# A state-space scan beside windowed attention: attention weights turned by DMA, local states evicted into their final place, and a new order of issue

## The chip, the cores and the metric

The kernel runs on one core of a Trainium2 chip. Times are device microseconds (us) of that core. The kernel before took 139.39 us, the median of three runs (138.95 to 139.60). A core has engines with queues of their own: TensorE (PE) for matmuls, VectorE (DVE), ScalarE (ACT), GpSimd (POOL) and SyncE (SP), which here only issues DMAs. Each engine works through its own instructions in the order in which they were issued, and waits on semaphores for the others.

## The reference

Two independent layers over 2048 positions of width 448, whose outputs stand side by side.

```
A: Lam_bar = exp(dt * Lam); B_bar = ((Lam_bar - 1) / Lam)[:, None] * Bmat
   h[t] = Lam_bar * h[t-1] + x[t] @ B_bar.T            (448 complex states, 2048 steps)
   y = 2 * (h @ Cmat.T).real + x * Dskip
B: q, k, v = split(x @ wqkv)                           (16 heads of 28)
   logits[s, w] = q[s] . k[s - 2w] / sqrt(28),  w = 0..7;  -1e9 where s - 2w < 0
   o = sum_w softmax(logits)[w] * v[s - 2w];    out = o @ wo
```

## The kernel before

Position s is written as (p, j) with s = 16 p + j: 128 chunks p, 16 places j in each. Most tiles hold one of them on the partitions, and j in the free dimension.

**Layer B.** x is loaded with transposing DMAs and projected to queries and keys on PE, with the chunks in the free dimension (`prep`). For half b of the places (8 each), `qk` builds products query × key on DVE, two windows at a time. `summ` (L658) sums them per head on PE into `logits`, a PSUM tile with eight windows of 128 columns; its partition is 32 i + 16 r + h for place i, group parity r and head h. Products pass through three buffers. `softmax(b)` then runs a chain: a mask matmul, the maximum over windows on DVE (`top`, L694), its subtraction on PE, the exponential on ACT, the sum over windows on PE (`tot`, L708), and reciprocal and scaling on DVE (`norm`, L713). The weights then have heads on the partitions, while the weighted sum needs chunks there. So `tr` (L720) turns the eight windows by eight PE transposes into a PSUM tile, and `ev` (L725) copies it to `attn` with two ACT copies. `v_proj` makes v per place and evicts it to `vd`, on ACT or DVE; `halo` (L773) shifts rows of `vd` by one chunk with DMAs for places before the first. `pv` multiplies weights and v and adds on DVE (L818, L821), the main work of DVE in the second half; `trd` (L855) transposes a group's result by DMA, or PE does for the last group (`tr`, L864), and PE multiplies with wo.

**Layer A.** Seven blocks m of 64 complex states. `scan` projects x (`bf`, `br`) into four PSUM tiles per block, one per residue i of the place modulo 4, and combines them in a logarithmic scan of matmuls with powers of the transition (`powers` on DVE, L1181) and ACT evictions between them. The projections of residues 0 and 2 are local states: they are evicted to a buffer `eP` (`evP`, L1250, or `evp`, L1253), used by `s1` (L1256), added back into PSUM through an identity matmul (`back`, L1322) once the carry is known, completed by `s6` and `s7`, and evicted for good into `h` (L1336, L1339). `h` has a tile of its own for m < 3; for m = 3 to 6 it lies over the queries of B. `outputs` multiplies h with C, adds the skip term, and evicts into a ring of eight rows for the output DMAs.

**Order.** A planner collects units (an engine, a cost, a function, what they depend on). When the list `ORDER` (L48) has as many entries as there are units, `run` (L130) issues the units in that order: an entry is the unit's number as created, and adding 1000 picks the second of two allowed engines. That order is the order in every engine's queue. Semaphores come from the data that the instructions touch.

SP's queue holds all loads: B's x and weights, A's x (L980, last at L983 to L984), C (L1006), wo (L402), halos, wo's second copy (L407), the Dskip row for A's skip term (L949, L951), the transpose of C (L1010), then transposes of results and the outputs. DVE's queue runs the projections' evictions, then products, `top`, `norm`, and `pv` with `powers` between its steps.

Of the kernel before, what the change touches and what calls it, by code (L numbers as in the profile page):

```python
# [9 lines left out]
ACT = mybir.ActivationFunctionType  # L10
# [28 lines left out]
NF = 3  # L39
WARM = 6  # L40
# [4 lines left out]
HOLD = (0, 0, 0, 1, 0, 0, 7)  # L45
YG = ((3,), (7,), (11,), (1, 5), (9,), (0, 4), (8,), (2, 6), (10,), (12, 13), (14,), (15,))
# [159 lines left out]
class Ctx:  # L206
# [41 lines left out]
    def consts2(self):  # L248
# [22 lines left out]
        def masks():  # L271
            G.memset(mrow[:], 0.0)
            G.affine_select(out=mrow[:], in_=mrow[:], compare_op=ALU.not_equal, fill=-1e9,
                            base=-3, pattern=[[1, 4]], channel_multiplier=1)
# [42 lines left out]
class PartB:  # L317
# [262 lines left out]
    def qk(self, b, prio):  # L580
# [8 lines left out]
        for g in (2 * b + 1, 2 * b):  # L589
            par = g - 2 * b  # L590
            j0 = 4 * g
            for tp in (3, 2, 1, 0):
# [65 lines left out]
                def summ(g=g, tp=tp, par=par, ub=ub, head=first):  # L658
# [5 lines left out]
                    zs = slice(H - H * par, 3 * H - H * par)  # L664
                    for kt in range(3):
                        for i in range(4):
                            nc.tensor.matmul(lg[32 * i:32 * i + 32, 2 * tp:2 * tp + 2, :],  # L667
                                             lhsT=cx.Z[:, kt, zs], rhs=pr[:, :, i, kt, :],
                                             start=(new and kt == 0), stop=(kt == 2), skip_group_check=True)
                    if tp < 2:  # L670
                        for z, t2 in ((cx.Z[:, 3, zs], tp + 2), (cx.Zh[:, zs], tp)):
                            for i in range(4):
                                nc.tensor.matmul(lg[32 * i:32 * i + 32, 2 * t2:2 * t2 + 2, :],
# [16 lines left out]
    def softmax(self, b, prio):  # L690
# [29 lines left out]
        def tr():  # L720
            pt = box["pt"] = self.psum.tile([NCH, W, 2, 4, H], bf16, name="pt_at", tag="s")
            for w in range(W):
                nc.tensor.transpose(pt[:, w].rearrange("q r i h -> q i r h"), box["a"][:, w, :], cx.ident[:])

        def ev():  # L725
            at = self.attn[b] = pool.tile([NCH, W // 2, 2, 2, 4, H], bf16, name="attn%d" % b)
            for x in range(2):
                nc.scalar.copy(at[:, 2 * x:2 * x + 2].rearrange("q z r y i h -> q y (z r) (i h)"),
                               box["pt"][:, 4 * x:4 * x + 4].rearrange("q (y z) r i h -> q y (z r) (i h)", y=2))
# [6 lines left out]
        u = P.add("PE", pe(8, 128), tr, [u], -1, acq="s", rel="at")  # L736
        self.u_attn[b] = P.add("ACT", 2 * act(512), ev, [u], -1, rel="s")

    def v_proj(self, prio, deps):
# [42 lines left out]
        for i0, i1 in ((10, 14), (6, 10), (2, 6), (0, 2)):  # L782
            z = P.add("POOL", 0.9, lambda i0=i0, i1=i1: zero(i0, i1), deps, prio[0])
# [5 lines left out]
    def pv(self, b, prio, deps):  # L789
# [12 lines left out]
        lasts = {}  # L802
        for r in (1, 0):
            last = getattr(self, "pv_last", None)
            us = (5, 4, 1, 0)
            for n in range(4):

                def step(n=n, r=r, part=0):
# [13 lines left out]
                    if n == 0:  # L822
                        mul(0)
                        mul(1)
# [3 lines left out]
                    elif 2 * b + r > 0:  # L828
                        add(3)
                        V.tensor_tensor(acc[:, n1:2 * n1], acc[:, 0:n1], acc[:, n1:2 * n1], op=ALU.add)  # L830
# [16 lines left out]
            if not hasattr(self, "u_first"):  # L847
                self.u_first = last
# [723 lines left out]
```

## Time and profile before

| what | us |
|---|---|
| median of three runs | 139.39 |
| the profiled execution | 139.57 |
| its span, first to last instruction | 137.9 |
| PE busy | 132.2 |
| DVE busy | 123.9 |
| ACT busy | 89.9 |
| POOL busy | 17.4 |

The profiled execution takes 1.7 us more than its span, for what lies around the instructions. Busy time counts an engine as busy while any of its instructions is under way; matmuls overlap, and their ends are modelled, so a busy PE is not one at its peak. A line such as `52.05 0.50 PE L1242 ... x2 [0.32 <-DMA ...]` of the timeline says when instructions of one kind started, how long they took together, where they stand in the program, how many they are, and how long the engine had been idle before, with what ended that idle time. The granted TensorE clock is 1.00 in this execution.

### The profile page before, as it was taken

How to read it: one execution, taken by the hardware profiler on the slowest of the kernel's cores; microseconds unless marked ns; L12 is line 12 of the kernel's file. 1: busy time of each engine (PE TensorE's matmuls, PEld its weight loads, DVE VectorE, ACT ScalarE, POOL GpSimd, SP SyncE). 2: the span in 40 equal slices, each digit the busy share in tenths (PEclk: the TensorE clock that was granted, in tenths of full speed). 3: DMA queues.
4: the chain of work that ended last, by engine and by line, in shares of the span. 5: the costliest groups of instructions: out<-in, count | busy, mean ns of one | idle time of the engine just before them, and what ended most of it. 6: DMA issues, size and time to landing. Idle time of an engine off the chain costs nothing.

```text
span 137.9 us, 2856 instructions
## 1 busy us (share of the span) xinstructions
PE 132.2 (96%) x1080; PEld 69.1 (50%) x1087; DVE 123.9 (90%) x135; ACT 89.9 (65%) x202; POOL 17.4 (13%) x69
## 2 busy tenths in 40 slices
PE   7999989999999998999999999999999999999990
PEld 2644334544555453656534664554665655445750
DVE  1379999899999999999999999999999999999950
ACT  3365588998553975856685899887746352463571
POOL 7489810018000000000000000000000000000000
PEclk9999999999999999999999999999999999999999
DMA  4968953564744337835799109800000462917554
GB/s 129 266 129 212 175 89 39 126 159 109 73 95 86 77 71 125 150 69 143 226 190 221 50 0 96 208 0 2 0 5 0 110 156 37 236 56 238 195 168 140
DMA packets 39582, 16.05 MB, mean 116 GB/s; under 512 B 31573, under 2 KB 38932, under 8 KB 39569
## 3 DMA queue, kind: packets, MB, share of 16 engines
q1 hardware_dynamic: 39506, 15.87, 53.6%
q8 instruction: 8, 0.13, 0.4%
q14 instruction: 5, 0.04, 0.1%
q10 hardware_dynamic: 63, 0.01, 0.0%
HBM read 4.32 MB, written 3.67 MB: 58 GB/s over the span
## 4 chain that ended last, share of the span: by engine, by line
PE 56%; SPq 34%; ACT 3%; issue 2%; DMA 2%; ACTq 0%
PE y_ps L1435 15%; SPq L980 14%; SPq L362 10%; PE scb L1233 6%; PE wo_ps L894 5%; PE scp L1233 3%; PE wo_ps L901 2%; PE scb L1292 2%; DMA xaT_sb<-in_A_x_dram 2%; PE scP L1233 2%; PE y_ps L1431 2%; PE scb L1257 2%; SPq L341 2%; SPq L365 2%; PE logits L667 1%
## 5 line engine op out<-in xcount | busy, mean ns | idle before, releaser
L818 DVE TENSOR_TENSOR prods<-attn,vd 128x3584 bf16<-128x3584 bf16 x12 | 24.1, 2020 | 0.0
L821 DVE TENSOR_TENSOR rb<-rb,prods 128x3584 bf16<-128x3584 bf16 x11 | 22.2, 2021 | 0.1
L652 DVE TENSOR_TENSOR prods<-qk 128x3072 bf16<-128x3072 bf16 (+1 forms) x15 | 19.2, 1328 | 0.3 <-PE logits L667 0.3
L1435 PE MATMUL y_ps<-Ccat,qk 128*128 128x448 bf16 x60 | 15.1, 353 | 0.1
L215 ACT CAST qk<-wo_ps 128x448 bf16<-128x448 f32 (+1 forms) x16 | 8.2, 528 | 10.1 <-PE wo_ps L894 6.5
L477 PE MATMUL qk_ps<-rb 128*128 128x512 bf16 x60 | 14.4, 379 | 0.4 <-DMA rb<-in_B_x_dram 0.4
L215 ACT CAST vd<-v_ps 128x448 bf16<-128x448 f32 x15 | 7.4, 539 | 5.8 <-PE v_ps L763 4.5
L1435 PE MATMUL y_ps<-Ccat,h 128*128 128x448 bf16 x45 | 11.0, 353 | 0.0
L1233 PE MATMUL scb<-xaT_sb,Bcat 128*128 128x512 bf16 x42 | 10.9, 381 | 0.0
L1233 PEld LDWEIGHTS <-Bcat 128*128 128x128 bf16 x84 | 7.6, 100 | 6.4 <-issue 0.2
L1285 ACT CAST ubuf<-scb 128x64 bf16<-128x64 f32 x35 | 7.1, 218 | 5.6 <-PE scb L1292 3.5
L763 PE MATMUL v_ps<-rb 128*128 128x448 bf16 x48 | 9.9, 353 | 0.0
L217 ACT ACTIVATE qk<-qk_ps 64x512 bf16<-64x512 f32 (+1 forms) x15 | 8.9, 599 | 1.0 <-PE qk_ps L484 0.5
L656 DVE TENSOR_TENSOR prods<-qk 128x768 bf16<-128x768 bf16 (+3 forms) x18 | 9.1, 569 | 0.3 <-ACT qk L215 0.2
L477 PEld LDWEIGHTS <-rb 128*128 128x128 bf16 x60 | 5.7, 98 | 7.3 <-issue 1.0
L1435 PEld LDWEIGHTS <-qk 128*128 128x128 bf16 x60 | 5.9, 98 | 5.3
L818 DVE TENSOR_TENSOR rb<-attn,vd 128x3584 bf16<-128x3584 bf16 x4 | 8.1, 2021 | 0.1
L894 PE MATMUL wo_ps<-wo_p,rb 128*128 128x448 bf16 x36 | 8.1, 354 | 0.0
L1183 DVE TENSOR_TENSOR pw<-Dm,spair 128x1920 bf16<-128x1920 bf16 x7 | 8.1, 1153 | 0.0
L215 ACT CAST qk<-qk_ps 128x512 bf16<-128x512 f32 (+2 forms) x11 | 6.3, 585 | 2.5 <-PE qk_ps L484 1.1
L1233 PE MATMUL scp<-xaT_sb,Bcat 128*128 128x512 bf16 x30 | 7.9, 380 | 0.0
L667 PE MATMUL logits<-prods,Zsel 128*32 128x256 bf16 x192 | 7.4, 274 | 0.0
(198 smaller groups left out, 263.1 us busy)
## 6 DMA issues: line engine op xcount, KB each, us to landing
out_dram<-qk SPq DMA_DIRECT2D x32, 112.0 KB, 1.8
vd<-vd SPq DMA_DIRECT2D x3, 392.0 KB, 4.4
rb<-in_B_wqkv_dram SPq DMA_DIRECT2D x3, 336.0 KB, 4.5
qk<-in_A_x_dram SPq DMA_DIRECT2D x1, 448.0 KB, 4.9
ra<-in_A_B_re_dram SPq DMA_DIRECT2D x1, 392.0 KB, 4.1
ra<-in_A_B_im_dram SPq DMA_DIRECT2D x1, 392.0 KB, 5.8
rb<-in_A_C_re_dram SPq DMA_DIRECT2D x4, 98.0 KB, 2.8
rb<-in_A_C_im_dram SPq DMA_DIRECT2D x4, 98.0 KB, 3.1
```

What stands on the lines that cost most here:

```text
L215: nc.scalar.copy(out, in_)
L362: nc.sync.dma_start(self.xT[:, j], bass.AP(x.tensor, x.offset + j * D - DT, [[T * D, NCH], [1, KT * NCH]]), transpose=True)
L477: nc.tensor.matmul(out(n), lhsT=w(n, full, k), rhs=self.xT[:, j:j + 4, k, :], start=(not rfirst and k == 1), stop=(rfirst and k == KT - 1) ...
L652: V.tensor_tensor(out.rearrange("p i j k q -> p i (j k) q"), qq.unsqueeze(1).to_broadcast([NCH, 2, 4 * nk, NCH]), bass.AP(kk.tensor, kk.of ...
L656: V.tensor_tensor(jk(out[:, i, a:e]), qq, kk, op=ALU.mult)
L763: nc.tensor.matmul(box["ps"][:].rearrange("p h d -> p (h d)"), lhsT=self.xT[:, j, k, :], rhs=self.wv[:, k, :], start=False, stop=(k == KT ...
L818: V.tensor_tensor(tmp[i].rearrange("p (j d h) -> p j d h", j=8, d=DH), aa, self.vd[:, o:o + 8], op=ALU.mult)
L821: V.tensor_tensor(acc, acc, tmp[i], op=ALU.add)
L894: nc.tensor.matmul(ps[:], lhsT=self.oTd[g][:, a + kt], rhs=self.wo_p[:, 5 * e + kt, :], start=False, stop=(kt == 2), skip_group_check=True)
L980: nc.sync.dma_start(self.xT[:, j], bass.AP(x.tensor, x.offset + j * D, [[T * D, NCH], [1, KT * NCH]]), transpose=True)
L1233: mt(box[i], lhsT=self.Bcat[:, k, m, :], rhs=self.xk(slice(i, None, 4), k), start=(i % 2 == 0 and k == 0), stop=False, **kw)
L1435: nc.tensor.matmul(ps, lhsT=h, rhs=self.Ccat[:, m, :], start=(m == 0 and not skip), stop=(m == NM - 1), skip_group_check=True)
```

## The change

**Logits.** The eight windows are stored in another order within `logits`, so that a pair of windows stands two apart; the mask follows. Matmuls, columns and banks stay as they are.

**Attention weights.** `tr` and `ev` are replaced by `turn`: per half, one transposing DMA on SP from the scaled weights (128 partitions, 8 windows of 128) into `attn`. `attn` gets the layout that this DMA writes, and the multiplication in `pv` reads it with other strides.

**Local states.** `evP` and `evp` write into rows 0 and 2 of `h`; `s1` and `back` read them there; the final evictions write the same rows. The buffer `eP` is gone.

**Switches.** `ADD` and `EADD` would let POOL DMAs with accumulation replace some additions. All their entries are zero, and `half` is None, so no instruction comes of them.

```
@@ qk.summ @@
+                    at = lambda t, i: lg[32 * i:32 * i + 32, 4 * (t // 2) + t % 2:4 * (t // 2) + t % 2 + 3:2, :]
...
-                            nc.tensor.matmul(lg[32 * i:32 * i + 32, 2 * tp:2 * tp + 2, :],
+                            nc.tensor.matmul(at(tp, i),
...
@@ softmax @@
-        def tr():
-            pt = box["pt"] = self.psum.tile([NCH, W, 2, 4, H], bf16, name="pt_at", tag="s")
-            for w in range(W):
-                nc.tensor.transpose(pt[:, w].rearrange("q r i h -> q i r h"), box["a"][:, w, :], cx.ident[:])
-
-        def ev():
...
+        def turn():
+            at = self.attn[b] = pool.tile([NCH, W, 4, 2, H], bf16, name="attn%d" % b)
+            nc.sync.dma_start(at[:].rearrange("q w i r h -> q w (i r h)"), box["a"][:].rearrange("p w q -> p (w q)"), transpose=True)
...
-        u = P.add("PE", pe(8, 128), tr, [u], -1, acq="s", rel="at")
-        self.u_attn[b] = P.add("ACT", 2 * act(512), ev, [u], -1, rel="s")
+        self.u_attn[b] = P.add("SP", 1.3, turn, [u], -1, rel="at", lat=3.0)
@@ pv.step.mul @@
-                        aa = self.attn[b][:, 2 * (u // 4) + u % 2, r].rearrange("q y i h -> q (y i) h").unsqueeze(2).to_broadcast(
+                        w0 = 4 * (u // 4) + 2 * (u % 2)
+                        aa = self.attn[b][:, w0:w0 + 2, :, r, :].rearrange("q y i h -> q (y i) h").unsqueeze(2).to_broadcast(
@@ scan @@
-            def evp(n, box=box, etile=etile):
-                nc.scalar.copy(etile()[:, n, :], box[2 * n])
+            def evp(n, box=box, hget=hget):
+                nc.scalar.copy(hget()[:, 2 * n, :], box[2 * n])
...
-                mt(box[1 + 2 * i], lhsT=L(1), rhs=box["eP"][:, i, :], start=False, stop=True, **kw)
+                mt(box[1 + 2 * i], lhsT=L(1), rhs=hget()[:, 2 * i, :], start=False, stop=True, **kw)
...
-                mt(box[2 * n], lhsT=cx.ident[:], rhs=box["eP"][:, n, :], start=True, stop=False, **kw)
+                mt(box[2 * n], lhsT=cx.ident[:], rhs=hget()[:, 2 * n, :], start=True, stop=False, **kw)
```

**Order.** There is one unit less per half, so later unit numbers shift. Up to the last load of A's x on SP and the same point on the other engines the order is as before. Behind it:

- SP, before: C, wo, halo of places 0–2, wo's second copy, Dskip (layout for the diagonal), halos 10–14 and 2–6, transpose of C, halo 6–10, transpose of group 3, then the Dskip row and x for the last four places of A, then outputs with the transposes of groups 2 and 1. After: Dskip (diagonal), wo, halos 0–2 and 10–14, the turn of half 1, C, halo 6–10, wo's second copy, transpose of C, transpose of group 3, x for the last places, halo 2–6, the turn of half 0, outputs and the other two transposes. The Dskip row goes out behind the output of place 10 of A.
- DVE, before, from the last eviction of keys: products (group, windows pair) 3/0, 3/1, 2/2, 2/0, 2/1, 1/3, `top` of half 1, an eviction of v (place 1), 0/3, 1/2, `norm` of half 1, 1/1, 0/1, 0/0, 1/0, 0/2, `powers` of block 3, `top` of half 0, `pv`. After: 2/0, 3/0, 2/1, 2/2, 3/1, 1/1, `top` of half 1, 1/3, 1/0, `powers` 3, 0/0, 0/1, 0/2, `norm` of half 1, 0/3, 1/2, `top` of half 0, `pv`. The eviction of v for place 1 is on ACT. Further on, `norm` of half 0 and `powers` of block 5 stand a few steps later in `pv`.
- PE: sums of products follow the products' new order; `tot` of half 1 stands behind the first steps of blocks 0 and 1 of the scan instead of ahead of them; blocks 2 and 3 alternate more closely, and block 4 is finished beside block 6; at the end the wo matmuls of place 7 stand behind the first closing transposes.
- ACT follows; the evictions of places 11 and 7 of B stand behind the first closing one.

More of the change, by code (lines that the diff above doesn't have):

```diff
@@ L39 @@
 NF = 3
+NC = 3
 WARM = 6
@@ L45 @@
 HOLD = (0, 0, 0, 1, 0, 0, 7)
+ADD = (0, 0, 0, 0, 0, 0, 0)
+EADD = (0, 0, 0, 0)
 YG = ((3,), (7,), (11,), (1, 5), (9,), (0, 4), (8,), (2, 6), (10,), (12, 13), (14,), (15,))
@@ L272, in masks @@
             G.memset(mrow[:], 0.0)
-            G.affine_select(out=mrow[:], in_=mrow[:], compare_op=ALU.not_equal, fill=-1e9,
-                            base=-3, pattern=[[1, 4]], channel_multiplier=1)
+            v = mrow[:].rearrange("p (z y) -> p y z", z=2)
+            G.affine_select(out=v, in_=v, compare_op=ALU.not_equal, fill=-1e9,
+                            base=-3, pattern=[[2, 2], [1, 2]], channel_multiplier=1)
             G.memset(mcol[:], 1.0)
@@ L782, in v_proj @@
         for i0, i1 in ((10, 14), (6, 10), (2, 6), (0, 2)):
-            z = P.add("POOL", 0.9, lambda i0=i0, i1=i1: zero(i0, i1), deps, prio[0])
+            z = P.add("POOL", 0.9, lambda i0=i0, i1=i1: zero(i0, i1), [*deps, *self.u_pad.values(), self.u_pad3, self.u_pad3b], prio[0])
             h = P.add("SP", 1.45, lambda i0=i0, i1=i1: halo(i0, i1), [self.u_v[i + 2] for i in range(i0, i1)],
@@ L801, in pv, with step @@
         n1 = 4 * D
-        lasts = {}
+        self.oTd = getattr(self, "oTd", {})
+        lasts, halves, trs = {}, {}, {}
         for r in (1, 0):
             last = getattr(self, "pv_last", None)
+            half = getattr(self, "u_half", None)
+            ahead = half is not None
             us = (5, 4, 1, 0)
             for n in range(4):
-                def step(n=n, r=r, part=0):
+                def step(n=n, r=r, part=0, half=half):
                     alloc()
@@ L822, in step @@
                     if n == 0:
+                        mul(1 if half else 0)
+                        mul(2 if half else 1)
+                    elif n == 1 and half:
+                        mul(3)
                         mul(0)
-                        mul(1)
+                    elif n == 2 and half:
+                        add(1)
+                        add(2)
                     elif n < 3:
@@ L829, in step @@
                         add(3)
-                        V.tensor_tensor(acc[:, n1:2 * n1], acc[:, 0:n1], acc[:, n1:2 * n1], op=ALU.add)
+                        if not EADD[2 * b + r]:
+                            V.tensor_tensor(acc[:, n1:2 * n1], acc[:, 0:n1], acc[:, n1:2 * n1], op=ALU.add)
                     else:
@@ L834, in pv @@
                 dd = []
-                for u in us[:2] if n == 0 else us[n + 1:n + 2] if n < 3 else ():
+                for u in us[:2 + ahead] if n == 0 else us[n + 1 + ahead:n + 2 + ahead] if n < 3 else ():
                     o = j0 + 4 * r + DIL * u
@@ L846, in pv, with merge @@
             self.pv_last = last
+            g = 2 * b + r
+            halves[g] = self.u_half = None
+            if EADD[g]:
+                def merge(g=g):
+                    acc = self.acc[g]
+                    nc.gpsimd.dma_start(acc[:, n1:2 * n1], acc[:, 0:n1], accum_op=ALU.add)
+                halves[g] = self.u_half = P.add("POOL", 1.1, merge, [last], PRI["wo"], lat=3.5)
             if not hasattr(self, "u_first"):
                 self.u_first = last
-        self.oTd = getattr(self, "oTd", {})
-        trs = {}
         for r in (1, 0):
@@ L858, in trd @@
                     nc.sync.dma_start(t, self.acc[g][:, n1:2 * n1], transpose=True)
-                trs[r] = P.add("SP", 1.7, trd, [lasts[r][1]], PRI["wo"], lat=3.6)
+                trs[r] = P.add("SP", 1.7, trd, [halves[g] or lasts[r][1]], PRI["wo"], lat=3.6)
         for j in range(j0, j0 + JB):
@@ L1305, in ev3, with carry @@
                 nc.scalar.copy(hget()[:, 3, 0:384], box[3][:, 0:384])
-            def carry(out, lt, Sc, hv):
-                mt(out[:, 0:NCH], lhsT=lt, rhs=Sc, start=False, stop=True, **kw)
+            def carry(out, lt, Sc, hv, new=False):
+                mt(out[:, 0:NCH], lhsT=lt, rhs=Sc, start=new, stop=True, **kw)
                 mt(out[:, NCH:512], lhsT=lt, rhs=hv[:, 3, 0:384], start=False, stop=True, **kw)
@@ L1390, in scan @@
             done[m] = P.add("POOL", 0.0, lambda: None, [w0, w2, u1], rel=("fl", "pw"), lat=0.0)
+            if add:
+                w0 = w2 = P.add("POOL", 1.2, addin, [w0, w2], pc, rel="cP", lat=3.0)
             self.u_h.append((w0, u1, w2, [u3, eh]))
```

61 lines of the change are left out of this document (33 added, 28 removed), and 56 rows, old and new, of the table ORDER.

## The prediction

> **What bounds the kernel now.** I read the page first: busy shares, then the chain that ended last.
>
> ```profile
> span 137.9 us, 2856 instructions
> PE 132.2 (96%) x1080; PEld 69.1 (50%) x1087; DVE 123.9 (90%) x135; ACT 89.9 (65%) x202; POOL 17.4 (13%) x69
> PE 56%; SPq 34%; ACT 3%; issue 2%; DMA 2%; ACTq 0%
> ```
>
> TensorE (PE) and VectorE (DVE) are both nearly full, so the page alone does not say which sets the end. The chain has two halves: SyncE's queue (SPq 34%) first, PE afterwards. Next I read the timeline of each engine where the halves meet and where the kernel ends (columns: start, duration, engine, line, operation, count; idle time before it in brackets).
>
> ```profile
> 49.11 1.28 SPq L980 DMA_TRANSPOSE xaT_sb<-in_A_x_dram  x1
> 52.05 0.50 PE L1242 MATMUL scb<-xaT_sb,Bcat 64*128 64x512 bf16 x2 [0.32 <-DMA xaT_sb<-in_A_x_dram]
> ...
> 98.02 0.73 PE L1435 MATMUL y_ps<-Ccat,h 128*128 128x448 bf16 x3
> ...
> 127.16 2.09 DVE L833 TENSOR_TENSOR rb<-rb,prods 128x1792 bf16<-128x1792 bf16 x2
> 128.09 1.49 PE L1435 MATMUL y_ps<-Ccat,S 128*128 128x448 bf16 x7
> 129.41 1.50 PE L870 MATMUL pt_o<-ident,rb 128*128 128x128 bf16 x24
> 134.43 0.53 ACT L215 CAST qk<-wo_ps 128x448 bf16<-128x448 f32 x1 [0.22 <-PE wo_ps L901]
> ```
>
> Two things are to be seen. At 52.05 PE waits for the last load of A's x, whose order the change keeps: PE time lost before that point is partly absorbed there. At the end, DVE's last add finishes at 129.25, PE's last y matmul at 129.58, and the closing work (pt_o, wo, eviction) starts from both. After 52 us the two engines thus run to the same finish; a gain on one alone is worth only what the other allows. So I costed DVE and PE apart.
>
> ```profile
> 52.10:65.20 13.10, 12.89 (x171) 7.57 (x174) 12.62 (x16) 8.72 (x27) 0.00 (x0) 1.00 0.65 123
> 97.00:118.00 21.00, 20.95 (x160) 12.25 (x161) 20.74 (x13) 9.79 (x21) 0.00 (x0) 1.00 0.29 52
> 65.20:129.30 64.10, 63.62 (x40) 1.00 0.46 105
> ```
>
> (Windows. The first two rows give length, then busy time and count of PE, PEld, DVE, ACT, POOL, the clock, DMA share, GB/s; the third gives DVE alone.) From 65.2 to 129.3 DVE idles 0.48 us in all: its finish is fixed by when the first weighted product starts. That start is the number to find.
>
> **The change, part by part.**
>
> *Removed from PE and ACT.* Per half of the sequence, eight transposes and two copies.
>
> ```profile
> 56.81 0.61 PE L723 MATMUL pt_at<-ident,attn_t 128*128 128x128 bf16 x8
> 57.64 1.08 ACT L728 COPY attn<-pt_at 128x512 bf16<-128x512 bf16 x2
> ```
>
> The eight transposes stand 0.45 us apart from the next work in the chain of waits (0.61 shown, their ends overlap), so PE saves 2 × 0.45 = 0.9 us and ACT 2 × 1.08 = 2.2 us. ACT is 65% busy; its saving is worth nothing by itself.
>
> *Local states written to their final place.* The evictions at L1251 and L1254 keep their count and shape and only change destination; the final eviction overwrites them after the matmuls that read them, as it already followed those. States 3 to 6 lie over the queries, whose last reader ended at 62.77 (below), before their first eviction. Cost 0 to 0; the switches ADD and EADD are all zero, so what they guard issues nothing.
>
> *The attention turn on SP.* One DMA per half moves 128 × 1024 elements, eight 128 × 128 blocks. No such DMA is in this trace; its nearest rows:
>
> ```profile
> xaT_sb<-in_A_x_dram SPq DMA_TRANSPOSE x16, 2.9
> rb<-rb SPq DMA_TRANSPOSE x3, 3.9
> Ccat<-rb SPq DMA_TRANSPOSE x1, 6.2
> vd<-vd SPq DMA_DIRECT2D x3, 392.0 KB, 4.4
> ```
>
> (Last number: median microseconds from issue to landing.) Four blocks land in 2.9, fourteen in 3.9, twenty-eight in 6.2. The bounds are 2.9 and 6.2; I take 3.9, the row with the same source memory and the nearer size. That is 3.9/14 = 0.28 us per block with all fixed latency included. The Trainium skill (VectorE: DVE Perf Modes, "The three transpose paths") gives 1309 ns for one such block by DMA against 390 ns on TensorE, and advises TensorE where PSUM will do; by it eight blocks in turn would take an estimated 10.5 us. The three rows contradict that as a price per block in a row of them.
>
> When can it be issued? SP in the new order does, after A's x: the Dskip row loads (3 DMAs), wo (8), halo 0–2, halo 10–14, then the turn, then C, which is moved behind it.
>
> ```profile
> 50.50 2.71 SPq L1006 DMA_DIRECT2D rb<-in_A_C_re_dram  x4
> ...
> 56.02 5.31 SPq L402 DMA_DIRECT2D wo_p<-in_B_wo_dram  x8
> 61.42 0.58 SPq L776 DMA_DIRECT2D vd<-vd  x1
> 62.05 0.98 SPq L777 DMA_DIRECT2D vd<-vd  x1
> ...
> 64.39 0.46 SPq L949 DMA_DIRECT2D dsk_raw<-in_A_Dskip_dram  x1
> 64.91 0.53 SPq L951 DMA_DIRECT2D dsk_raw<-in_A_Dskip_dram  x2
> 65.47 0.55 SPq L776 DMA_DIRECT2D vd<-vd  x1
> 66.07 0.86 SPq L777 DMA_DIRECT2D vd<-vd  x1
> ```
>
> From 50.5: Dskip 1.05, wo 5.4, halos 1.6 and 1.5 give 60.1. Landing 60.1 + 3.9 = 64.0 (63.0 to 66.3). C goes out from about 61 instead of 50.5 and is needed by the first y matmuls at 98.02: some 30 us of cover for its loads and its own transpose. The second turn: between its weights and their first reader stand five DVE instructions of 2.02 (row of 65.16 below), 10 us, so 3.9 is covered by 6. While SP waits for those weights, the output of j = 14 and the transpose of group 2 stand behind; the latter needs a later add anyway.
>
> *DVE's order from 30.4 to the first weighted product.*
>
> ```profile
> 30.41 1.90 DVE L656 TENSOR_TENSOR prods<-qk 128x768 bf16<-128x768 bf16 x3 [0.21 <-ACT qk L215]
> 44.60 0.61 DVE L219 CAST vd<-v_ps 128x448 bf16<-128x448 f32 x1
> 45.45 3.70 DVE L656 TENSOR_TENSOR prods<-qk 128x768 bf16<-128x768 bf16 x6
> 58.60 1.76 DVE L652 TENSOR_TENSOR prods<-qk 128x3072 bf16<-128x3072 bf16 x1 [0.31 <-PE logits L667]
> 61.02 1.75 DVE L652 TENSOR_TENSOR prods<-qk 128x3072 bf16<-128x3072 bf16 x1
> 62.69 1.15 DVE L1183 TENSOR_TENSOR pw<-Dm,spair 128x1920 bf16<-128x1920 bf16 x1
> 63.34 0.50 PE L667 MATMUL logits<-prods,Zsel 128*32 128x256 bf16 x12
> 63.77 0.20 PE L286 MATMUL logits<-mrow,mcol 128*128 128x4 bf16 x2
> 64.02 1.22 DVE L696 TENSOR_REDUCE mx<-logits 128x128 bf16<-128x1024 f32 x1 [0.17 <-PE logits L286]
> 65.16 2.02 DVE L818 TENSOR_TENSOR rb<-attn,vd 128x3584 bf16<-128x3584 bf16 x1
> ```
>
> The same instructions run between 30.4 and 65.16 in another order, less one: the eviction of v for j = 1 goes to ACT (44.60 to 45.13, so −0.53). The product now first (r = 0, windows 7 and 6) needs keys of half 1 alone, so the wait of 0.21 goes. The 0.31 goes too, as TensorE's sums now stand closer behind their products. What comes: in the old order the power build (62.69, 1.15 long) lay between the last product and the second maximum and covered its logits on PE. It now runs earlier, and the maximum follows the last product directly. Old distance 62.77 to 64.02 = 1.25, with a backlog of sums on PE; the new one has one sum (twelve matmuls, a 0.50 row) and the mask (0.20), with a handover either side: I take 0.95, bounds 0.7 and 1.25. Against the old idle 0.17 that is +0.78 (0.53 to 1.08). Second, the row sums of half 1 on PE move behind the first steps of scan blocks 0 and 1. Those cannot start before the 52.05 of the x loads and took up to the transposes at 56.81 in the old trace, while DVE reaches the reciprocal at about 57.1: a wait of 0 to 0.6, I take 0.3.
>
> Sum for DVE: −0.53 − 0.21 − 0.31 + 0.78 + 0.3 = 0.0 (−0.5 to +0.6). The first weighted product stays at 65.2. Back from it: maximum 1.14, wait 0.95, two products 3.65; so the weights are ready for the turn at about 59.5, SP is free at 60.1, and the turn lands at 64.0. It is hidden, with 1.2 us to spare. If that cover were gone, each microsecond would go to the end in full. The reads at L818 keep runs of 16 elements and get another stride between them: I count nothing, 0 to 0.
>
> *PE after 52.* It is released at the second maximum by the same products, so it stands level there, then saves the second 0.45. Also the wo matmuls of j = 7 move behind the first closing transposes:
>
> ```profile
> 128.33 0.97 ACT L215 CAST qk<-wo_ps 128x448 bf16<-128x448 f32 x2 [1.63 <-PE wo_ps L894]
> ```
>
> Three matmuls 0.19 apart (seven of the same width in the 1.49 at 128.09) are 0.56. The first closing transposes come at 129.41 − 0.45 − 0.56 = 128.4, just as DVE's first half of the last add is done. PE no longer holds the end up; DVE does. From the last add, I lay the closing steps out with the durations of the old ones (eight transposes 0.45, as 24 in 1.50; four wo matmuls 0.75; evictions 0.53): the last eviction ends 5.3 us after it, against 134.96 − 129.25 = 5.7 before. That is −0.4. ACT has two more evictions in this tail (j = 11 and 7, 0.53 each); they fit between the steps.
>
> The Dskip row for the final y now goes out behind the output of y 10, whose matmuls stand some 8 us of PE work before the closing transposes; with its eviction that puts the issue near 122.7. Before, it landed in 4.9:
>
> ```profile
> rb<-in_A_Dskip_dram SPq DMA_DIRECT2D x1, 112.0 KB, 4.9
> 129.17 1.08 DVE L1412 TENSOR_TENSOR qk<-qk,rb 128x1792 bf16<-128x1792 bf16 x1
> ```
>
> At 127.6 it is there 1.5 us before its reader.
>
> *Sum.* 0.0 on DVE, −0.4 at the end: span 137.5, and the profiled execution's 139.57 becomes 139.2. That execution lies 0.18 above the median of the runs, 139.39; against the median I forecast 139.0. With 0.5% (0.7 us) as what a measurement can tell, that is no change, leaning faster.
>
> **The rivals.**
>
> *Denser than counted.* The waits I put in at the maximum and the reciprocal come to 0.7 and 0, so DVE gains 0.55, and the tail 0.4: 138.4. For it: PE gives up 0.9 and ACT 2.2 in the scan stage, where ACT steps wait for PE and back. Against it: one sum must still run after the last product.
>
> *The turn lands late (slower).* Its bytes go out on the same queue behind a halo of 392 KB whose kind takes 4.4 us. If landing takes more than 5.1 us from its issue, DVE waits, and the surplus goes to the end; the sum changes sign from 5.5. With 6.2, the row of Ccat, and one more microsecond of queueing it lands at 67.3: +2.1 − 0.4 = 140.9 or so; at 6.2 alone, 139.9. For it: the halo ahead. Against: the fourteen-block transposes took 3.9. The Trainium skill (DMA: Bandwidth & Descriptors, "Queues, rings and completion order") says that a DMA's semaphore write lands only after every earlier write of that DMA engine; by that rule the halo's last bytes delay the turn, which speaks for this rival, and no run here isolates it yet.
>
> *Each block in turn.* If the eight blocks cost 1.31 us each, as mechanism a serial walk through blocks, landing is 70.6 and DVE starts 5.4 late: 144. The skill's page above would have it so; 0.28 per block in the row of rb says no.
>
> *PE becomes the bound.* The scan blocks 2 and 3 now alternate, 4 ends later. If PE's gaps between 65 and 128 grow by 1.9 us or more, the end follows PE: 140 and up.
>
> *It doesn't do what it says.* The transposes removed were fill for PE while ACT worked, and PE just waits instead: then only the tail moves, which is my sum with 0.2 less: 139.2.
>
> **How the numbers follow.** My sum, with the last rival, 50%, own range 138.4 to 139.6; of it 15 points lie beyond 0.5% faster. Denser 21%, nearly all beyond 0.5%. Late turn 17%, PE bound 9%, serial blocks 3%: of these 26 points beyond 0.5% slower, 3 within. So faster 0.36, same 0.38, slower 0.26. The range 137.9 to 140.6 takes in the denser case and half of the late ones.
>
> **What would show it.** Right: no pt_at at L723, two DMA transposes into attn landing in 3 to 4.5 us; the first product from attn at 64.8 to 65.8 with no wait for a DMA; DVE idle near 1 us before its second maximum; the first pt_o before 128.8. Wrong: DVE's first read of attn released by the DMA (late turn), PE idle in the scan rows and y matmuls running past DVE's last add (PE bound), or L818 no longer at 2.02 us.

## The result

The changed kernel takes 140.1 us (median of 6 runs, 139.79 to 140.38), against 139.43 us for the kernel before beside it (6 runs, 138.95 to 139.74): ratio 1.0051, 95% interval 1.0027 to 1.0075. It is slower by about half a per cent. The profiled execution took 140.0 us, with a span of 138.3. Three of the four runs of one experiment below (C ahead of the turn) were taken at a lower granted clock, 0.974 to 0.988, than all other runs of this study (0.995 or more), and are not compared with them.

The page of the changed kernel, the same three lines as were shown of before:

```profile
span 138.3 us, 2835 instructions
...
PE 131.3 (95%) x1065; PEld 67.2 (49%) x1071; DVE 123.0 (89%) x134; ACT 88.3 (64%) x199; POOL 17.7 (13%) x69
...
DVE 39%; PE 38%; SPq 9%; issue 5%; ACT 3%; DMA 3%; DVEq 0%; ACTq 0%
```

PE, DVE and ACT all do less than before (PE 131.3 against 132.2, DVE 123.0 against 123.9, ACT 88.3 against 89.9), and yet the span is 0.4 us longer. The chain of work that ended last has changed: PE 56% and SyncE's queue 34% before, now DVE 39% and PE 38%. This does not yet say where the time goes; the timeline has to. The next rows are the changed kernel's timeline, for the places on which the prediction's steps rested, then its waits on SyncE's queue and its DMA issues.

```profile
56.82 0.95 DVE L720 RECIPROCAL rsum<-sm_ps 128x128 f32<-128x128 f32 x1
59.13 1.50 SPq L727 DMA_TRANSPOSE attn<-attn_t  x1
63.51 1.22 DVE L701 TENSOR_REDUCE mx<-logits 128x128 bf16<-128x1024 f32 x1 [0.80 <-PE logits L290]
64.65 2.02 DVE L819 TENSOR_TENSOR rb<-attn,vd 128x3584 bf16<-128x3584 bf16 x1
...
126.48 2.09 DVE L841 TENSOR_TENSOR rb<-rb,prods 128x1792 bf16<-128x1792 bf16 x2
```

```profile
SPq L727 <- DVE attn_t L722: 5.4, 2, 3.9
```

```profile
attn<-attn_t SPq DMA_TRANSPOSE x1, 3.1
```

The front of the kernel went as forecast, or a little better. The first weighted product starts at 64.65 (65.16 before), no DMA holds it up, and the last add ends at 126.48 + 2.09 = 128.57 instead of 129.25: in this pair of traces DVE has gained 0.68 us. Kernels with the same front differ by up to 0.5 us here (in the nine traces of this study with the new front the last add ends between 128.44 and 128.93, in the three with the old one between 128.90 and 129.25), so the gain is rather 0.5, the difference of the means. The loss is behind that point. The timeline of the changed kernel's tail (three engines; columns as before):

```profile
121.25 1.50 PE L1462 MATMUL y_ps<-Ccat,S 128*128 128x448 bf16 x7
...
127.63 0.51 PE L884 MATMUL pt_o<-ident,rb 128*128 128x128 bf16 x6
128.63 0.29 PE L884 MATMUL pt_o<-ident,rb 128*128 128x128 bf16 x2 [0.49 <-DVE rb L841]
128.76 0.73 PE L908 MATMUL wo_ps<-wo_p,rb 128*128 128x448 bf16 x3
129.32 0.61 PE L884 MATMUL pt_o<-ident,rb 128*128 128x128 bf16 x8
130.46 0.92 PE L915 MATMUL wo_ps<-wo_p,rb 128*128 128x448 bf16 x4 [0.52 <-ACT qk L218]
131.21 0.61 PE L884 MATMUL pt_o<-ident,rb 128*128 128x128 bf16 x8
131.98 0.61 PE L884 MATMUL pt_o<-ident,rb 128*128 128x128 bf16 x8 [0.17 <-DVE qk L1474]
...
128.49 1.08 DVE L1439 TENSOR_TENSOR qk<-qk,rb 128x1792 bf16<-128x1792 bf16 x1
129.78 2.15 DVE L1474 TENSOR_TENSOR qk<-y_ps,qk 128x448 bf16<-128x448 f32 x3 [0.20 <-DVE qk L1439]
...
128.96 0.59 ACT L889 CAST rb<-pt_o 128x512 bf16<-128x512 f32 x1 [3.89 <-PE pt_o L884]
129.44 0.97 ACT L218 CAST qk<-wo_ps 128x448 bf16<-128x448 f32 x2
134.94 0.53 ACT L218 CAST qk<-wo_ps 128x448 bf16<-128x448 f32 x1 [0.23 <-PE wo_ps L915]
```

The same stretch before, of PE and DVE:

```profile
130.75 0.92 PE L901 MATMUL wo_ps<-wo_p,rb 128*128 128x448 bf16 x4
131.51 0.61 PE L870 MATMUL pt_o<-ident,rb 128*128 128x128 bf16 x8
...
130.46 2.15 DVE L1447 TENSOR_TENSOR qk<-y_ps,qk 128x448 bf16<-128x448 f32 x3 [0.20 <-DVE qk L1412]
```

From the end of the last add to the end of the last eviction, the tail, are 135.47 − 128.57 = 6.90 us; before there were 5.71, and the forecast said 5.3. DVE's gain and the tail's loss of 1.19 together make the half microsecond of the traces. In this stretch PE, which had no gap there before, stands idle three times (0.49, 0.52, 0.17), and ACT stands idle for 3.89 us ahead of the first closing eviction, with the eviction of j = 11, whose wo matmuls were done at 127.67, queued behind it.

### The profile page after: what moved, and what is told of

It is laid out like the page before. It is cut to its first block, busy times and chain, and to the rows that moved or that the text cites. A ratio compares the mean times of both kernels' runs of the same rounds, so it can differ in the third digit from the quotient of the medians.

```text
span 138.3 us, 2835 instructions
## 1 busy us (share of the span) xinstructions
PE 131.3 (95%) x1065; PEld 67.2 (49%) x1071; DVE 123.0 (89%) x134; ACT 88.3 (64%) x199; POOL 17.7 (13%) x69
## 4 chain that ended last, share of the span: by engine, by line
DVE 39%; PE 38%; SPq 9%; issue 5%; ACT 3%; DMA 3%; DVEq 0%; ACTq 0%
DVE rb L822 11%; DVE prods L819 11%; SPq L366 6%; PE v_ps L760 6%; PE scb L1247 5%; DVE rb L819 4%; PE scp L1247 4%; PE logits L672 3%; DMA rb<-in_B_x_dram 3%; DVE pw L1197 2%; PE qk_ps L481 2%; DVE prods L656 2%; PE wo_ps L915 2%; DVE rb L838 2%; ACT qk L218 1%
## 5 line engine op out<-in xcount | busy, mean ns | idle before, releaser
L819 DVE TENSOR_TENSOR prods<-attn,vd 128x3584 bf16<-128x3584 bf16 x12 | 24.0, 2018 | 0.0
L1462 PE MATMUL y_ps<-Ccat,qk 128*128 128x448 bf16 x60 | 14.6, 352 | 0.0
L218 ACT CAST vd<-v_ps 128x448 bf16<-128x448 f32 x16 | 7.9, 540 | 5.2 <-PE v_ps L760 4.9
L218 ACT CAST qk<-y_ps 128x448 bf16<-128x448 f32 (+1 forms) x9 | 5.6, 663 | 8.2 <-issue 4.2
```

Of the source, the lines that this page charges most:

```text
L218: nc.scalar.copy(out, in_)
L819: V.tensor_tensor(tmp[i].rearrange("p (j d h) -> p j d h", j=8, d=DH), aa, self.vd[:, o:o + 8], op=ALU.mult)
L1462: nc.tensor.matmul(ps, lhsT=h, rhs=self.Ccat[:, m, :], start=(m == 0 and not skip), stop=(m == NM - 1), skip_group_check=True)
```

## The experiments

Four theories. **1**, the order of ACT's queue: the evictions of j = 11 and 7 stand behind the first closing eviction, and ten evictions in a row then set the tail. **2**, a dependency that the data does not need: the transposes of place 1 read columns up to 960, the last add is cut at 896, so two of them wait for the wrong half (the 0.49). **3**, banks of PSUM, the memory into which PE writes: this kernel gives six banks in turn to PE's results, and a result keeps its bank until another engine has evicted it, that is, copied it out. y of places 15 and 14 hold banks until DVE evicts them, after the last add and the Dskip product (x times Dskip for the last places), and closing work (transposes and wo of places 0 to 3) has to wait for these. **4**, the turn or the states in place cost something themselves.

For reading the diffs, units of the order list: 586 and 587 are the transposes and eviction of place 1, 591 and 592 of place 2, 597 and 598 of place 3, 581 and 582 of place 0; 588 is the closing wo of place 1; 555 and 556 are eviction and output of j = 11, 613 to 615 wo, eviction and output of j = 7; 682 are the seven matmuls of y 15, 683 its eviction, 676 and 680 those of y 12/13 and y 14. Line numbers of the experiments are shifted by some lines.

**j = 11's eviction ahead**

```diff
-    675, 554, 586, 587, 555, 556, 613, 614, 615, 591, 592,
+    675, 554, 555, 556, 586, 587, 613, 614, 615, 591, 592,
```

> Only the eviction and the output of j = 11 are moved ahead of the first closing transposes and their eviction. Theory 1 (the order of ScalarE's queue): in the changed kernel j = 11's wo result is ready at about 127.6, but its eviction stands behind the first closing eviction, for which ScalarE idles 3.89 us; moved, it runs in that idle time, ScalarE's tail is one eviction of 0.53 us shorter, and the time falls by about 0.5 us to 139.6. Theory 2 (the last two of the first closing transposes wait for the wrong half of the last add) and theory 3 (the y evictions on VectorE hold the banks of PSUM): no change, within 0.2 us.

Measured: 139.81 us (12 runs), ratio to before 1.0031 (1.0012 to 1.0049). ACT's row of this eviction moved into the idle stretch as planned; the first closing wo did not move with it. Timeline of this run:

```profile
130.56 0.92 PE L918 MATMUL wo_ps<-wo_p,rb 128*128 128x448 bf16 x4 [0.52 <-DVE qk L1477]
...
129.88 2.15 DVE L1477 TENSOR_TENSOR qk<-y_ps,qk 128x448 bf16<-128x448 f32 x3 [0.20 <-DVE qk L1442]
```

The wait is again 0.52, and with ACT's work gone the row now names another releaser: DVE's y eviction.

**j = 7's wo, eviction and output ahead as well**

```diff
-    675, 554, 586, 587, 555, 556, 613, 614, 615, 591, 592,
+    675, 554, 555, 556, 613, 614, 615, 586, 587, 591, 592,
```

> As the run before, and j = 7's wo matmuls, eviction and output are moved ahead too, as the kernel before had them. Theory 1: two evictions (1.1 us) leave ScalarE's tail, and TensorE's wait of 0.52 us for a bank that j = 7's eviction gives back goes: last eviction ends near 134.2 instead of 135.47, time about 138.9 (-1.2). Theory 2: the first closing transposes still wait for the second half of the last add, so at most -0.4. Theory 3: no change, within 0.2 us.

Measured: 139.73 us (12 runs), ratio 1.0029 (1.0007 to 1.0052). Timeline of this run:

```profile
130.81 0.92 PE L918 MATMUL wo_ps<-wo_p,rb 128*128 128x448 bf16 x4 [1.09 <-DVE qk L1477]
...
126.84 2.09 DVE L844 TENSOR_TENSOR rb<-rb,prods 128x1792 bf16<-128x1792 bf16 x2
...
130.13 2.15 DVE L1477 TENSOR_TENSOR qk<-y_ps,qk 128x448 bf16<-128x448 f32 x3 [0.20 <-DVE qk L1442]
134.93 0.53 ACT L221 CAST qk<-wo_ps 128x448 bf16<-128x448 f32 x1 [0.23 <-PE wo_ps L918]
```

Two evictions have left ACT's tail, and the last eviction still ends at 135.46. PE's wait has grown from 0.52 to 1.09 by what was saved ahead of it. Theory 1 falls as the cause of the loss: it expected 138.9. A gain of 0.3 to 0.4 us may be real, but the intervals of the two ratios overlap that of the changed kernel.

**The last add cut at column 960**

```diff
-  a, t = (v.rearrange("p (y j c) -> p y j c", y=2, j=4)[:, :, 2 * part:2 * part + 2] for v in (acc, tmp[3]))
+  a, t = (v.rearrange("p (y c) -> p y c", y=2)[:, :, (0, 960)[part]:(960, 1792)[part]] for v in (acc, tmp[3]))
```

> Only the cut of the last add moves, from column 896 to column 960 of 1792; the first closing transposes read up to column 960. Theory 2: the last two of them no longer wait for the second half (0.49 us of wait in the changed kernel), the first closing eviction starts about 0.9 us earlier and the time falls by 0.5 us or more, to 139.6 or less. Theory 1: the first eviction starts earlier, but ten evictions in a row still follow, and TensorE waits for them: it gets some of that too, 0.3 to 0.6 us, so this run alone does not part it from theory 2; the pair with the next run does. Theory 3: within 0.2 us.

Measured: 140.14 us (8 runs), ratio 1.0066 (1.0043 to 1.009). Timeline of this run:

```profile
127.56 0.62 PE L884 MATMUL pt_o<-ident,rb 128*128 128x128 bf16 x8
...
130.32 0.92 PE L915 MATMUL wo_ps<-wo_p,rb 128*128 128x448 bf16 x4 [1.13 <-DVE qk L1474]
...
129.64 2.15 DVE L1474 TENSOR_TENSOR qk<-y_ps,qk 128x448 bf16<-128x448 f32 x3 [0.20 <-DVE qk L1439]
```

The wait of 0.49 is gone: all eight transposes run at once. Nothing is gained, because the time reappears at the closing wo (1.13). Theory 2 described a real wait, but a later one takes up what it gives.

**Both**

> Both: j = 11's and j = 7's closing work ahead of the first closing transposes, and the last add cut at column 960. If theories 1 and 2 both hold, their gains add up to 1.5 to 1.8 us: last eviction near 133.8, time 138.3 to 138.6, below the kernel before. If theory 2 is empty, it equals the run without the moved cut. Theory 3: within 0.3 us of the changed kernel. If the order elsewhere had cost the kernel its time (theory 4: the turn or the states in place), this run would stay above the kernel before.

Measured: 139.82 us (12 runs), ratio 1.0042 (1.0021 to 1.0064). Timeline of this run:

```profile
130.67 0.92 PE L918 MATMUL wo_ps<-wo_p,rb 128*128 128x448 bf16 x4 [1.20 <-DVE qk L1477]
...
129.99 2.15 DVE L1477 TENSOR_TENSOR qk<-y_ps,qk 128x448 bf16<-128x448 f32 x3 [0.20 <-DVE qk L1442]
```

The gains do not add (138.3 to 138.6 was expected for that), and the five traces share one distance: the first closing wo starts 0.68 us after the first y eviction starts (129.78 to 130.46, 129.88 to 130.56, 130.13 to 130.81, 129.64 to 130.32, 129.99 to 130.67), whatever ACT does. The eviction of y 15, the first of the three in that row, takes 0.62 us by itself, so the wo starts 0.05 us behind its end. The program as built says why. The result tile of that wo lies in PSUM bank 2, which y 15 holds, and its first matmul waits for y 15's eviction; the last transposes lie in y 14's bank. In the kernel before, that result lies in bank 7, which an eviction by ACT empties; only the fourth group of transposes (131.51 above) and a later wo result follow y evictions, and they start without a wait. y 15's seven matmuls moved from 128.09 to 121.25: seven microseconds earlier into a bank that DVE cannot empty before 130.4. Theory 3 is the one left, and the next two runs test it by exchange.

**The changed kernel with the old order of the tail**

```diff
-    602, 609, 682, 603, 604, 616, 623, 605, 610, 618, 611, 612, 669, 606, 679, 607, 608, 675, 554, 586, 587,
...
+    616, 554, 555, 679, 669, 556, 623, 609, 602, 613, 610, 603, 675, 606, 682, 614, 615, 586, 611, 607, 604,
...
```

> The changed kernel, its last 52 units of work (from j = 4's and 5's first wo matmuls on) put into the order that the kernel before has for them. In the changed kernel y of place 15 is computed at 121.25 instead of 128.09 and holds its PSUM bank until VectorE has done the last add and the Dskip product; the first closing wo matmul writes to that bank and starts 0.68 us after that eviction starts, in all five kernels with the new tail. Theory 3 (PSUM banks that wait for VectorE's y evictions): in this order the bank of that matmul comes from an eviction on ScalarE, the tail from the last add to the end takes 5.7 us as before instead of 6.9, the last add still ends near 128.6, and the time is about 138.9, below the kernel before. Theory 4 (turn or states in place cost something themselves): the time stays at 139.4 or above, though the wait is gone.

Measured: 138.83 us (12 runs), ratio 0.9961 (0.9939 to 0.9984). Timeline of this run:

```profile
126.81 1.49 PE L1465 MATMUL y_ps<-Ccat,S 128*128 128x448 bf16 x7
128.13 1.72 PE L887 MATMUL pt_o<-ident,rb 128*128 128x128 bf16 x24
129.69 0.92 PE L918 MATMUL wo_ps<-wo_p,rb 128*128 128x448 bf16 x4
...
126.52 2.09 DVE L844 TENSOR_TENSOR rb<-rb,prods 128x1792 bf16<-128x1792 bf16 x2
...
133.41 0.53 ACT L221 CAST qk<-wo_ps 128x448 bf16<-128x448 f32 x1 [0.22 <-PE wo_ps L918]
```

No closing wo waits. The last add ends at 128.61, the last eviction at 133.94: a tail of 5.33 us, better than the 5.7 expected for this run and as the prediction had it. That the time is within 0.2 us of its 139.0 is partly luck, as DVE's term came out better than it said. Everything in the change but the order of these 52 units is still there, and it is now faster than before.

**The exchange the other way**

The kernel before, with the changed kernel's order of the same units at its end.

> The exchange the other way: the kernel before, with the changed kernel's order for the same 52 units. Nothing else of the change is in it. Theory 3: the last add ends at 129.25 as before; the first closing wo matmul waits for y 15's eviction (from 130.46, so it starts near 131.1 instead of 130.75), the transposes of place 0 wait for y 14's, which is third now (near 132.65), and the last eviction ends 3.5 us after those begin, at 136.1 instead of 134.96: time about 140.6, slower by 1.2 us. Theory 4: 139.4, no change.

Measured: 140.78 us (6 runs), ratio 1.0123 (1.0092 to 1.0154). The time came out as expected, but by chance, not by the expected path. Timeline of this run:

```profile
122.06 0.73 PE L1438 MATMUL y_ps<-Ccat,h 128*128 128x448 bf16 x3 [1.55 <-ACT qk L218]
...
130.22 0.61 PE L873 MATMUL pt_o<-ident,rb 128*128 128x128 bf16 x8
...
129.33 1.09 DVE L1415 TENSOR_TENSOR qk<-qk,rb 128x1792 bf16<-128x1792 bf16 x1 [0.43 <-DMA rb<-in_A_Dskip_dram]
```

PE lost 1.55 us at 120.5, where it waited for an eviction by ACT (it starts at 121.07, behind five others back to back): in the program as built y of places 12 and 13 goes into the one PSUM tile for pairs, which that eviction empties. PE reached the closing transposes at 130.22, so late that the banks of theory 3 were free; DVE's Dskip product, too, waited 0.43 us for its row. The list transplanted into another context made a new wait of its own. This run says that the order is worth more than a microsecond; it is no test of the bank of y 15.

**One unit moved**

So the bank was tested with one unit: the run with j = 11 and j = 7 ahead (139.73), and y 15's matmuls moved behind them.

```diff
-    602, 609, 682, 603, 604, ...
-    675, 554, 555, 556, 613, 614, 615, 586, 587, 591, 592,
+    602, 609, 603, 604, ...
+    675, 554, 555, 556, 613, 614, 615, 682, 586, 587, 591, 592,
```

> The run with j = 11's and j = 7's closing work moved ahead (139.73), with one more unit moved: y 15's seven matmuls stand behind j = 5's wo, y 14, y 13 and the wo of 11 and 7, right ahead of the first closing transposes, as late as the kernel before has them. In the program as built the first closing wo result then lies in a bank that ScalarE empties (bank 6, j = 11's) instead of y 15's (bank 2), and only the last closing transposes follow a y eviction. Theory 3 (a bank held for VectorE): TensorE's wait of 1.09 us ahead of the first closing wo goes, the last eviction ends near 134.1, and the time is about 138.8, 0.9 us below the run without this move. If the gain of the old tail came from its other differences (three groups of transposes in a row, the order of the y evictions), this run stays within 0.3 us of 139.7.

Measured: 139.0 us (12 runs), ratio 0.9949 (0.992 to 0.9978), against 1.0029 (1.0007 to 1.0052) without the move. Timeline of this run:

```profile
126.99 1.49 PE L1465 MATMUL y_ps<-Ccat,S 128*128 128x448 bf16 x7
128.31 1.28 PE L887 MATMUL pt_o<-ident,rb 128*128 128x128 bf16 x16
129.83 0.93 PE L918 MATMUL wo_ps<-wo_p,rb 128*128 128x448 bf16 x4 [0.23 <-ACT rb L892]
...
126.71 2.09 DVE L844 TENSOR_TENSOR rb<-rb,prods 128x1792 bf16<-128x1792 bf16 x2
...
130.01 2.15 DVE L1477 TENSOR_TENSOR qk<-y_ps,qk 128x448 bf16<-128x448 f32 x3 [0.20 <-DVE qk L1442]
133.96 0.53 ACT L221 CAST qk<-wo_ps 128x448 bf16<-128x448 f32 x1 [0.23 <-PE wo_ps L918]
```

The same work, the same closing order; the closing wo now starts ahead of the y eviction, the wait of 1.09 is 0.23 and for ACT's eviction of its own input, and the last eviction ends 0.97 us earlier, 0.84 of it behind the last add (a tail of 5.69 against 6.53). Theory 3 is shown, for the kernel with 11 and 7 ahead; the same move on the changed kernel alone was not run.

**Three groups of transposes in a row, and then the cut at 960**

```diff
-    591, 592, 588, 589, 597, 683, 684, 590, 598, 676, 680, 677, 581, 582,
+    591, 592, 581, 582, 588, 589, 597, 683, 684, 590, 598, 676, 680, 677,
```

> As the run before, and the transposes of place 0 moved ahead of the first closing wo, so that three groups go in a row, as in the kernel before. No closing matmul but the last transposes waits for a bank of VectorE's. Theory 3: the wait is gone already, so this is within 0.3 us of the run before it, 138.5 to 139.0.

> As the run before, with the last add cut at column 960, so that the first closing transposes read only its first part. With the wait for banks gone TensorE sets the tail, and it reaches these transposes at about the time the last add ends (128.6): gain 0 to 0.2 us, 138.4 to 138.9. If the second theory's wait (0.49 us in the changed kernel) had been hidden only by the bank, 0.4 us or more.

Measured: 138.84 us (12 runs, ratio 0.9959, 0.994 to 0.9978) and, with the cut, 138.7 us (9 runs, ratio 0.9938, 0.9915 to 0.996). Neither step can be told from the one before it. The last has the lowest median of this study: 1.4 us below the changed kernel, 0.7 below the kernel before.

**The turn undone**

On the kernel with the old order of the tail (138.83), eight transposes on PE and two copies on ACT a half, at the place in the order where the DMA was.

```diff
-    nc.sync.dma_start(at[:].rearrange("q w i r h -> q w (i r h)"), box["a"][:].rearrange("p w q -> p (w q)"), transpose=True)
+    for w in range(W):
+        nc.tensor.transpose(pt[:, w].rearrange("q i r h -> q (i r h)"), box["a"][:, w, :], cx.ident[:])
...
+    for x in range(2):
+        nc.scalar.copy(at[:, 4 * x:4 * x + 4], box["pt"][:, 4 * x:4 * x + 4])
```

> The changed kernel with the old order of the tail, and the attention weights turned on TensorE and evicted by ScalarE again (eight transposes and two copies a half, the new layout kept). If the turn's worth is the 0.9 us that it takes off TensorE, and TensorE sets the end once the wait for banks is gone, this is 0.5 to 0.9 us slower than the same kernel with the turn. If the turn is worth nothing at the end, or VectorE alone sets it, within 0.2 us of it.

Measured: 140.65 us (6 runs), ratio 1.0096 (1.0073 to 1.012): the turn is worth 1.8 us in this order, twice what was expected. Timeline of this run, and the maximum in the run with the turn:

```profile
61.07 0.64 PE L731 MATMUL pt_at<-ident,attn_t 128*128 128x128 bf16 x8
61.74 1.08 ACT L736 COPY attn<-pt_at 128x512 bf16<-128x512 bf16 x2 [0.89 <-PE scb L1314]
62.87 0.37 PE L1266 MATMUL scb<-xaT_sb,Bcat 64*128 64x512 bf16 x1 [0.57 <-ACT attn L736]
65.17 1.23 DVE L704 TENSOR_REDUCE mx<-logits 128x128 bf16<-128x1024 f32 x1 [2.19 <-PE logits L293]
```

```profile
63.56 1.22 DVE L704 TENSOR_REDUCE mx<-logits 128x128 bf16<-128x1024 f32 x1 [0.84 <-PE logits L293]
```

In the new order the weights of half 1, which comes first, are ready only at 59.4, so the transposes stand right ahead of the sums of half 0. They take PE's time, and then PE waits another 0.57 for ACT's copies: in the program as built the next projection of the scan gets the bank that the transposes hold until they are copied. The maximum waits 2.19 us for its sums instead of 0.84, and these 1.35 us are most of the loss; 0.3 more was there before the transposes. It is the last maximum that prices the turn, not PE's busy time. Another place or another bank for the transposes was not tried, so the price is that of this order.

**C ahead of the turn**

```diff
-    526, 212, 246, 247, 302, ...  533, 283, 284, 152, 253, ...
+    526, 152, 212, 246, 247, 302, ...  533, 283, 284, 253, ...
```

> The changed kernel, C's eight loads issued ahead of the first turn on SyncE's queue instead of behind it; this takes away the cover that the prediction named for the turn. Their issue takes 5.6 us from 57.5 on, so the turn goes out at about 63.1 instead of 59.1 and lands near 66.2. The first weighted product, at 64.65 with the cover, waits for that DMA and starts near 66.3; by the rule that a microsecond lost there goes to the end in full, the time is 141.7 (+1.6). If a landing also takes longer behind C's bytes, up to 143. If the end is set by something else, below 140.6.

Measured: four runs, 142.43 to 145.63 us. Timeline and DMA issues of the run that took 145.63:

```profile
65.10 1.73 SPq L730 DMA_TRANSPOSE attn<-attn_t  x1
...
70.27 2.03 DVE L822 TENSOR_TENSOR rb<-attn,vd 128x3584 bf16<-128x3584 bf16 x1 [5.31 <-DMA attn<-attn_t]
```

```profile
attn<-attn_t SPq DMA_TRANSPOSE x1, 5.0
```

Without the cover the first product waits for the DMA. In this trace C's issue took 6.4 us instead of 5.6, and the turn landed 5.0 us after its issue instead of 3.1. The granted clock is 1.00 up to 84 us here, so the wait at 65 to 70 does not come of a lower clock; from 84 to 92 it is 0.77 to 0.81, and what that adds is not shown. So the size stays open: by the one run at a clock of 1.00 it is 2.3 us (142.43 against 140.1), between the expected 141.7 and 143. All four runs are slower than the changed kernel; where the run of 142.43 waits, no trace shows.

**The states in place alone**

The kernel before, with the local states evicted into their last place and its own order.

> The kernel before with one part of the change alone: the local states evicted into their last place, order of issue as before. The prediction put this at 0 to 0. Theory 4 (a cost of its own, from writes that lie over the queries or from the stride of the destination): above 139.9. Otherwise 139.2 to 139.6, no difference.

Measured: 139.71 us (12 runs), ratio 1.0023 (0.9992 to 1.0055). This lies between the two expectations. A difference is not shown, and up to half a per cent is not excluded; theory 4 is not supported for this part, and the turn, by the run above, gains.

## Why the prediction was wrong

It forecast 139.0 us, no change leaning faster; the kernel takes 140.1, inside the range of 137.9 to 140.6, but it is slower. By its own steps:

- *The step that failed* is the tail: "From the last add, I lay the closing steps out with the durations of the old ones ...: the last eviction ends 5.3 us after it ... That is −0.4." It took 6.90 us, +1.19 against before. The steps were laid out in the old closing order, with a free PSUM bank for each result. The new order computes y 15 seven microseconds earlier, a moved step that the prediction did not list; its bank stays taken until DVE evicts it after the last add and the Dskip product, and the first closing wo waits for that bank. With the old order of these units the tail takes 5.33 us and the kernel 138.83. By the tails of the traces, 6.90, 6.53 with 11 and 7 ahead, 5.69 with y 15 moved back as well, 5.33 in the old order: of the 1.57 us too many, 0.84 hang on this one result; the other two steps of 0.37 and 0.36 come of the rest of the closing order, and no run parts them further.
- "ACT has two more evictions in this tail ...; they fit between the steps." Moved out of the way together with 7's wo matmuls, they took 0.37 us off the tail of the trace and 0.4 off the median, with overlapping intervals: they are not the main loss, but that they fit is not shown.
- *DVE's order, 0.0 (−0.5 to +0.6)*: in the changed kernel's trace the first weighted product came at −0.5, as the rival "denser than counted" had it; over the traces of each front (64.52 to 65.01, nine of them, against 64.80 to 65.16, three) the means differ by 0.3, between the sum and the rival. The wait at the maximum was 0.80 (0.95 taken), the one at the reciprocal nothing (0.3 taken; the row at 56.82 has no idle time).
- *The turn's issue at 60.1, landing in 3.9*: issued at 59.13, landed in 3.1, and in 3.1 to 3.8 over the nine traces. SyncE was free earlier and waited for the weights (the two turns waited 5.4 us together, the longer 3.9, so the first 1.5); it was the weights and not the queue that set the time. That the turn is hidden was right, with 2.4 us to spare instead of 1.2, and the run with C ahead bears out the warning on its cover. The Trainium skill (VectorE: DVE Perf Modes, "The three transpose paths") gives 1309 ns for one 128 × 128 block; the trace has eight in 3.1 us. The same page ("Rules for kernel authors") advises TensorE if a destination in PSUM is OK; here the weights have to be copied on from PSUM, and that path cost 1.8 us in the new order. The Trainium skill's statement on completion order (DMA: Bandwidth & Descriptors, "Queues, rings and completion order") would fit the landing of 5.0 behind C's loads, but that is one trace, and no run parts it from mere traffic.
- *"ACT is 65% busy; its saving is worth nothing by itself"* and PE's 2 × 0.45: too low for the new order. There the scan, and behind it the sums of half 0, wait for the transposes and for ACT's copies of them; together they cost 1.35 us at the maximum.
- *States in place, 0 to 0*: no difference shown. *The products from attn at 2.02 us*: 2018 ns on average, right.
- The rivals that made it slower were late landing, serial blocks and a busy PE. None of them happened in the changed kernel. A resource that one engine holds for another, far from where it was filled, was not among them, although the closing work takes eight tiles (four of transposes, four of wo) from a ring of six banks that the y results of single places share.

## What to carry to other kernels

When an order of issue changes, list for every moved result not only when it is computed but which buffer it takes and who frees it when; a result computed early for an engine that comes late takes a bank from the closing work. Three of the waits found here were of this kind: for the bank of y 15, for the tile of a pair of y results, and for the bank of the attention transposes. A wait that is removed and leaves the time unchanged has a second wait behind it: look for a distance that stays the same in every variant (here 0.68 us from the y eviction to the wo), rather than trust the releaser that one row names. And a transplant of a whole order list proves little; moving a single unit made the point.

## What was not expected of the hardware

- A DMA transpose of eight 128 × 128 blocks between SBUF tiles landed in 3.1 us in the changed kernel, where the fourteen-block ones of before took 3.9, with 1.50 us on SyncE's queue for its issue. This is the turn of half 1, and it took 3.1 to 3.8 in nine traces; no landing is recorded for the other half. In the one trace with eight loads of 98 KB ahead of it, a run that took 145.63 us, it took 5.0.
- The eight loads of wo, 5.31 us of issue before, took 3.61 us in the changed kernel, in another place of the same queue; why, no run here isolates:

```profile
50.82 3.61 SPq L406 DMA_DIRECT2D wo_p<-in_B_wo_dram  x8
```
